# Converting streamed float64 weights: low halves moved from GpSimd to VectorE, casts as separate steps, products kept in PSUM

## The chip, the core and the metric

The kernel runs on one NeuronCore of a Trainium2 chip. The core has five instruction queues that run side by side and wait for each other through semaphores: TensorE (PE: matmuls into PSUM; PEld: its weight loads), VectorE (DVE), ScalarE (ACT), GpSimd (POOL), and SyncE (SP), which here only issues DMAs. Each queue runs its own instructions strictly in the order in which they were written. The metric is the device time of one execution in microseconds; lower is better.

## The reference, cut to what matters

A linear attention over 768 steps (a decaying 48 x 48 state per head), then two gated feed-forward layers, without any nonlinearity:

```python
# r, k, v: (4, 8, 768, 48) float32
for t in range(S):
    kt, vt, rt = (k[:, :, t], v[:, :, t], r[:, :, t])
    cur = np.einsum('bhd,bhe->bhde', u[None] * kt, vt)
    y[:, :, t] = np.einsum('bhd,bhde->bhe', rt, state + cur)
    state = w[None, :, :, None] * state + np.einsum('bhd,bhe->bhde', kt, vt)
...
x = y.transpose(0, 2, 1, 3).reshape(3072, 384)
x = ((x @ w_a) * (x @ w_b)) @ w_out          # w_a, w_b: 384 x 1536, w_out: 1536 x 384
out = ((x @ w1) * (x @ w2)) @ w3 @ w_out2    # w1, w2: 384 x 1024, w3: 1024 x 1024, w_out2: 1024 x 384
```

r, k, v, w and u arrive as float32, the seven weight matrices as float64.

## The kernel before, in words

**Precision.** A product of two float32 matrices is made of three fast matmuls: each operand is split into a high part (`hi`, the value rounded to fp32r, a cast) and a low part (`lo` = value - `hi`), and hi\*hi + lo\*hi + hi\*lo is summed in PSUM. So every weight and every intermediate needs a cast (ScalarE) and a subtraction.

**Conversion of weights (class `Stream`).** A weight arrives as float64 seen as pairs of 32-bit words, in jobs of 128 x 512 elements. The DMA (SP, L83) brings a job into a staging buffer `stg_t`; three VectorE instructions make a float32 of it in a buffer `cvt`: L98 (`shift`), L114 and L117 (`begin`). Then ScalarE casts it to `hi` (L136) and a subtraction gives `lo` (L137): on GpSimd for weights, on VectorE for the jobs that bring a float32 intermediate `m_d` back. Two more ScalarE instructions per job, Square (L121) and Sign (L139), each with an accumulator read, check the range of the values. `step()` is `finish()` of the oldest begun job (cast, low part, Sign, then the DMA of the next job), and `begin()` of the next one (L114, then L98 of the job behind it, L117, Square). `AHEAD` staging buffers are in flight. 61 jobs are float64 weights: 27 in the first stage (18 of w_a and w_b, `wab`, and 9 of w_out, `wout` and `wo`), the other 34 (`w12`, `wo2`, `w3`) from the last block of the first layer on.

**Stages.** Step 0 is the attention over the first 128 positions of the four batches (units u = 0 to 3; functions with `_0`). Then comes the first feed-forward layer in six blocks q of 512 tokens: for each of 12 feature tiles f TensorE makes a (9 matmuls, L635), b (9, L635) and, one f later, m (9 matmuls, L686 to L688, with `w_out`). Between them `merge` puts, as `side`, the attention of the next 128 positions (`unit_slots`: scores L367 and L383, `a_evac` L389, `a_diag` L395, `y_mm` L414/L419, `s_mm` L480), and as `late` the conversion steps: in block q = 0 the wab and wo jobs, in the last block the w12, wo2 and w3 jobs. The second layer runs over the same six blocks with w1/w2, and w3 @ w_out2 folded into one matrix (`fold`, L783).

**Per feature tile (`ab_slots`).** ScalarE copies a from PSUM to `g` (L654); VectorE multiplies it with b in PSUM (L660, result back into `g`, SBUF); ScalarE casts `g` to `gh` (L661); VectorE makes `gl` = `g` - `gh` (L666). TensorE's m waits for `gh` and `gl`. a and b live in three PSUM buffers `ab`. On GpSimd run the attention's elementwise products: `rk` (L321, L325), `kn` and `k` (L356), state decay `s` (L486), `pr` (L345, L347), from the third block on also `rbl` (L336) and `ktl` (L340).

**What sets the order.** The order on each queue is that of the Python code; `merge` spreads `side` and `late` evenly over the main slots. `STEPS_U`, `STEPS_K` and `TAIL` say how many conversion steps stand at each point of step 0. `st.split(n)` makes steps at once until the weights that TensorE needs next are there.

Of the kernel before, what the change touches and what calls it, by code (L numbers as in the profile page):

```python
# [23 lines left out]
DM = H * D  # L24
# [18 lines left out]
STEPS_K = (0, 2, 1, 0)  # L43
# [14 lines left out]
class Stream:  # L58
# [7 lines left out]
    AHEAD = 3  # L66

    def __init__(self, nc, stg, chk, small):
        self.nc, self.stg, self.chk, self.small = nc, stg, chk, small
        self.jobs, self.tiles = [], {}  # L70
        self.issued = self.shifted = self.begun = self.done = self.n64 = 0

    def add(self, src, dst, lo_eng=None):

        self.jobs.append((src, dst, lo_eng or self.nc.vector))
        return len(self.jobs)
# [13 lines left out]
    def shift(self):  # L90

        n = self.shifted
        if n == self.issued:
            return
        if self.jobs[n][0].dtype == I64:
            w = self.tiles[n].bitcast(I32).rearrange("p (n t) -> p n t", t=2)
            f = self.stg.tile([128, 512], I32, name="cvt", bufs=3)
            self.nc.vector.tensor_scalar(out=f, in0=w[:, :, 1], scalar1=3, scalar2=0x3FFFFFFF,  # L98
                                         op0=ALU.logical_shift_left, op1=ALU.bitwise_and)
            self.tiles[n] = (self.tiles[n], f)  # L100
        self.shifted += 1

    def begin(self):
# [7 lines left out]
        if self.jobs[n][0].dtype == I64:  # L111
# [43 lines left out]
def rwkv_moe_kernel(ctx, tc, rkT, nat, wu, wab, wout, w12, w3T, wo2, r_in, k_in, v_in, w_in, u_in, out):  # L155
# [10 lines left out]
    with tc.manual_schedule():  # L166
# [58 lines left out]
        def add_wab(i):  # L225
# [374 lines left out]
        for u in range(B):  # L600
# [10 lines left out]
            steps(STEPS_U[u])  # L611
            if u == 2:
# [25 lines left out]
        def ab_slots(x, wget, keep):  # L638
# [17 lines left out]
            def evac_b():  # L656
# [64 lines left out]
        def add_wo2(i):  # L721
# [5 lines left out]
            for j in range(3):  # L727
                s = slice(j * 512, (j + 1) * 512)
                st.add(flat(wo2)[:, i * 1536 + j * 512:][:, :512], lambda s=s: dst(s), nc.gpsimd)

        def add_w3(i):
# [5 lines left out]
            for j in range(2):  # L737
                s = slice(j * 512, (j + 1) * 512)
                w3_ready[i] = st.add(flat(w3T[i])[:, s], lambda s=s: dst(s), nc.gpsimd)

        lag, late = [], []
        for q in range(NB):
# [10 lines left out]
            if q == 0:  # L753
                late = [step] * (len(st.jobs) - st.begun + 1)
                late += [lambda: None] * (len(late) // LATE)
            if q == NB - 1:
# [7 lines left out]
                late = [step] * (len(st.jobs) - st.begun + 1)  # L764
# [65 lines left out]
        for q in range(NB):  # L830
# [29 lines left out]
            merge(main, [], late=[step] * (24 if q == 0 else 4) + [lambda: None] * (0 if q == 0 else 2))  # L860
# [254 lines left out]
```

## Time and profile before

| what | value |
|---|---|
| time, median of three runs (lowest to highest) | 942.9 us (940.86 to 945.25) |
| the profiled execution: its time / its span in the trace | 940.6 us / 938.9 us |
| TensorE busy, of the span | 898.6 us, 96% |
| VectorE / ScalarE / GpSimd busy | 478.8 / 344.0 / 306.5 us |
| chain that ended last, by engine | TensorE 80%, VectorE 11%, DMA 4%, issue 3% |
| mean granted TensorE clock | 0.979 |

The profiled execution lies 2.3 us below the median. The busy shares are means over stages that differ: in the page's 40 slices VectorE shows 7 to 9 tenths in the first six slices (up to about 140 us), mostly 4 to 5 over the next sixteen, 7 again from about 516 to 610 us, and 2 to 3 at the end. TensorE shows less than 9 in the first six slices and twice between 540 and 610 us, and the granted clock dips there too.

### The profile page before, as it was taken

How to read it: one execution, taken by the hardware profiler on the slowest of the kernel's cores; microseconds unless marked ns; L12 is line 12 of the kernel's file. 1: busy time of each engine (PE TensorE's matmuls, PEld its weight loads, DVE VectorE, ACT ScalarE, POOL GpSimd, SP SyncE). 2: the span in 40 equal slices, each digit the busy share in tenths (PEclk: the TensorE clock that was granted, in tenths of full speed). 3: DMA queues.
4: the chain of work that ended last, by engine and by line, in shares of the span. 5: the costliest groups of instructions: out<-in, count | busy, mean ns of one | idle time of the engine just before them, and what ended most of it. 6: DMA issues, size and time to landing. Idle time of an engine off the chain costs nothing.

```text
span 938.9 us, 12503 instructions
## 1 busy us (share of the span) xinstructions
PE 898.6 (96%) x4898; PEld 766.0 (82%) x4898; DVE 478.8 (51%) x684; ACT 344.0 (37%) x721; POOL 306.5 (33%) x245
## 2 busy tenths in 40 slices
PE   7778889999999999999999989899999999999997
PEld 7656678888888888888888867799988888888886
DVE  8799994545344544454442777765322222323222
ACT  4555653322322232223221775755422222222221
POOL 4566766555355626543420342322200000000000
PEclk9789889999999999999999999999999999999999
DMA  9534532212212211122102435443110010100001
GB/s 276 170 115 149 165 112 62 79 46 79 61 60 75 64 59 65 46 62 80 45 1 84 146 124 159 140 157 106 34 45 23 35 35 34 34 34 1 34 1 37
DMA packets 26065, 73.56 MB, mean 78 GB/s; under 512 B 3152, under 2 KB 7376, under 8 KB 26000
## 3 DMA queue, kind: packets, MB, share of 16 engines
q1 hardware_dynamic: 26000, 72.70, 24.6%
q8 instruction: 40, 0.66, 0.3%
q14 instruction: 25, 0.20, 0.1%
HBM read 61.28 MB, written 9.44 MB: 75 GB/s over the span
## 4 chain that ended last, share of the span: by engine, by line
PE 80%; DVE 11%; DMA 4%; issue 3%; ACT 1%; SPq 0%; DVEq 0%
PE ab L635 45%; PE m L686 4%; PE m L687 4%; PE m L688 4%; PE at L783 4%; DVE cvt L114 3%; PE o L807 3%; PE o L806 3%; PE o L808 3%; DVE cvt L117 2%; PE at L419 2%; PE at L414 2%; DVE cvt L98 1%; DMA stg_t<-in_wout_dram 1%; DVE gl L666 1%
## 5 line engine op out<-in xcount | busy, mean ns | idle before, releaser
L660 DVE TENSOR_TENSOR g<-g,ab 128x512 f32<-128x512 f32 x120 | 82.2, 685 | 269.1 <-PE ab L635 261.3
L635 PE MATMUL ab<-xt,w12h 128*128 128x512 f32 x576 | 177.5, 389 | 0.0
L661 ACT CAST gh<-g 128x512 fp32r<-128x512 f32 x120 | 74.5, 621 | 263.4 <-DVE g L660 263.4
L654 ACT COPY g<-ab 128x512 f32<-128x512 f32 x120 | 70.1, 584 | 247.4 <-PE ab L635 246.9
L666 DVE TENSOR_TENSOR gl<-g,gh 128x512 fp32r<-128x512 f32 x120 | 107.1, 893 | 65.0 <-ACT gh L661 65.0
L635 PEld LDWEIGHTS ab<-xt,w12h 128*128 128x128 f32 x576 | 107.5, 188 | 18.9
L635 PE MATMUL ab<-xt,w12l 128*128 128x512 f32 x288 | 112.0, 389 | 0.0
L687 PE MATMUL m<-gl,woh 128*128 128x512 f32 x216 | 86.4, 400 | 9.0 <-DVE gl L666 9.0
L686 PE MATMUL m<-gh,woh 128*128 128x512 f32 x216 | 87.3, 404 | 1.3 <-ACT gh L661 1.3
L336 POOL TENSOR_TENSOR rbl<-rk,rbh 48x512 fp32r<-48x512 f32 x32 | 49.3, 1542 | 120.1 <-ACT rbh L329 118.9
L688 PE MATMUL m<-gh,wol 128*128 128x512 f32 x216 | 85.2, 395 | 0.0
L635 PEld LDWEIGHTS ab<-xt,w12l 128*128 128x128 f32 x288 | 54.0, 188 | 11.2
L114 DVE SCALAR_TENSOR_TENSOR cvt<-stg_t,cvt 128x512 int32<-128x512 int32 x61 | 59.2, 970 | 0.3
L687 PEld LDWEIGHTS m<-gl,woh 128*128 128x128 f32 x216 | 41.3, 191 | 19.5 <-DVE gl L666 11.6
L117 DVE SCALAR_TENSOR_TENSOR cvt<-stg_t,cvt 128x512 int32<-128x512 int32 x61 | 54.5, 893 | 0.3
L686 PEld LDWEIGHTS m<-gh,woh 128*128 128x128 f32 x216 | 41.2, 191 | 12.4 <-ACT gh L661 3.3
L635 PE MATMUL ab<-xt,wab1h 128*128 128x512 f32 x144 | 47.0, 409 | 2.5 <-ACT wab1h L136 2.5
L688 PEld LDWEIGHTS m<-gh,wol 128*128 128x128 f32 x216 | 41.3, 191 | 8.7
L395 DVE COPY_PREDICATED a_sc<-ident,dg 128x512 f32<-128x512 int32 x40 | 46.3, 1197 | 0.0
L635 PE MATMUL ab<-xt,wab0h 128*128 128x512 f32 x144 | 45.3, 396 | 0.8 <-ACT g L654 0.8
L635 PE MATMUL ab<-xt,wab3h 128*128 128x512 f32 x144 | 45.9, 400 | 0.0
L635 PE MATMUL ab<-xt,wab2h 128*128 128x512 f32 x144 | 45.8, 400 | 0.0
(283 smaller groups left out, 1805.8 us busy)
## 6 DMA issues: line engine op xcount, KB each, us to landing
natt<-in_nat_dram SPq DMA_DIRECT2D x20, 576.0 KB, 5.0
rk<-in_rkT_dram SPq DMA_DIRECT2D x24, 448.0 KB, 4.2
stg_t<-in_wab_dram SPq DMA_DIRECT2D x18, 512.0 KB, 3.6
stg_t<-in_w3T_dram SPq DMA_DIRECT2D x16, 512.0 KB, 3.6
stg_t<-in_w_dram SPq DMA_DIRECT2D x12, 512.0 KB, 3.7
stg_t<-in_wout_dram SPq DMA_DIRECT2D x9, 512.0 KB, 3.5
m_d<-m_sb SPq DMA_DIRECT2D x18, 256.0 KB, 2.3
stg_t<-m_d SPq DMA_DIRECT2D x18, 256.0 KB, 2.6
```

Of the source, the lines that this page charges most:

```text
L114: nc.vector.scalar_tensor_tensor(out=f, in0=w[:, :, 1], scalar=-0x40000000, in1=f, op0=ALU.bitwise_and, op1=ALU.bitwise_or)
L117: nc.vector.scalar_tensor_tensor(out=f, in0=w[:, :, 0], scalar=29, in1=f, op0=ALU.logical_shift_right, op1=ALU.bitwise_or)
L336: eng.tensor_tensor(out=l, in0=rf_t[u][a:e], in1=h, op=ALU.subtract)
L395: nc.vector.copy_predicated(out=a_t[u][:, 4 * hf:4 * hf + 4, :], mask=ident.bitcast(I32).rearrange("p (o n) -> p o n", o=1).to_broadcast([ ...
L635: mm(ps, lhsT=w[i][:, k, cs], rhs=x[:, j, k, :], start=(n == 0), stop=(n == 3 * KD - 1))
L654: nc.scalar.copy(out=t["g"], in_=t["a"])
L660: nc.vector.tensor_tensor(out=g, in0=g, in1=t["b"], op=ALU.mult)
L661: nc.scalar.copy(out=gh, in_=g)
L666: nc.vector.tensor_tensor(out=gl, in0=t["g"], in1=gh, op=ALU.subtract)
L686: mm(m_ps[q][k], lhsT=wh[:, j, cs], rhs=gh, start=(f == 0), stop=False)
L687: mm(m_ps[q][k], lhsT=wh[:, j, cs], rhs=gl, start=False, stop=False)
L688: mm(m_ps[q][k], lhsT=wl[:, j, cs], rhs=gh, start=False, stop=(f == NF1 - 1))
```

## The change

Five things change.

1. In `Stream`, the low part of every job is made on VectorE (the argument that named an engine is gone). The 61 subtractions of the weights (L137) leave GpSimd.
2. Cast and Square become a step of their own, `cast()`, that stands behind each `step()` in the lists; `finish()` calls it only where it has not been made. `finish()` is now the low part and Sign.
3. `a*b` is written back into b's PSUM buffer; `gh` and `gl` are made from there.
4. Four staging buffers instead of three, and two `cvt` buffers instead of three.
5. In step 0, the loads of `k_0`, of `u_bc`, and of `rk` and `natt` for units 4 and 5 no longer stand ahead of all conversions' loads; `later_loads(u)` issues them behind units 0, 2 and 3. `STEPS_K` moves one step from unit 1 to unit 3.

```diff
-STEPS_K = (0, 2, 1, 0)
+STEPS_K = (0, 1, 1, 1)
...
-    AHEAD = 3
+    AHEAD = 4
...
-    def add(self, src, dst, lo_eng=None):
-
-        self.jobs.append((src, dst, lo_eng or self.nc.vector))
+    def add(self, src, dst):
+
+        self.jobs.append((src, dst))
...
-            f = self.stg.tile([128, 512], I32, name="cvt", bufs=3)
+            f = self.stg.tile([128, 512], I32, name="cvt", bufs=2)
...
+        self.begun += 1
+
+    def cast(self):
+
+        nc, n = self.nc, self.cast_
+        if n == self.begun:
+            return
+        hi, lo = self.jobs[n][1]()
+        if self.jobs[n][0].dtype == I64:
+            t, f = self.tiles[n]
+            f = f.bitcast(F32)
+            nc.scalar.copy(out=hi, in_=f)
             sq = self.stg.tile([128, 512], BF16, name="sq", bufs=1)
             high = t.bitcast(F32).rearrange("p (n t) -> p n t", t=2)[:, :, 1]
             nc.scalar.activation(out=sq, in_=high, func=ACTF.Square, accum_out=self.chk[:, self.n64, 0:1])
-            self.tiles[n] = (f.bitcast(F32), sq, self.n64)
+            self.tiles[n] = (f, hi, lo, sq, self.n64)
             self.n64 += 1
         else:
-            self.tiles[n] = (self.tiles[n], None, None)
-        self.begun += 1
+            f = self.tiles[n]
+            nc.scalar.copy(out=hi, in_=f)
+            self.tiles[n] = (f, hi, lo, None, None)
+        self.cast_ += 1
...
-        _, dst, eng = self.jobs[self.done]
-        t, sq, n = self.tiles.pop(self.done)
-        hi, lo = dst()
-        nc.scalar.copy(out=hi, in_=t)
-        eng.tensor_tensor(out=lo, in0=t, in1=hi, op=ALU.subtract)
+        if self.done == self.cast_:
+            self.cast()
+        f, hi, lo, sq, n = self.tiles.pop(self.done)
+        nc.vector.tensor_tensor(out=lo, in0=f, in1=hi, op=ALU.subtract)
...
-        nc.sync.dma_start(out=u_bc, in_=u_in.rearrange("(o h) d -> o (h d)", o=1).to_broadcast([128, DM]))
-        for u in range(B):
-            nc.sync.dma_start(out=k_0[:, u, :], in_=nat[u, :, 1, :])
-        for u in (B, B + 1):
-            load_rk(u)
-            load_nat(u)
+
+        def later_loads(u):
+            if u == 0:
+                for b in range(B):
+                    nc.sync.dma_start(out=k_0[:, b, :], in_=nat[b, :, 1, :])
+            elif u == 2:
+                load_rk(B)
+                nc.sync.dma_start(out=u_bc, in_=u_in.rearrange("(o h) d -> o (h d)", o=1).to_broadcast([128, DM]))
+                load_nat(B)
+            elif u == 3:
+                load_rk(B + 1)
+                load_nat(B + 1)
...
             for _ in range(n):
                 step()
+                st.cast()
...
             steps(STEPS_U[u])
+            later_loads(u)
...
-                nc.vector.tensor_tensor(out=g, in0=g, in1=t["b"], op=ALU.mult)
-                nc.scalar.copy(out=gh, in_=g)
+                nc.vector.tensor_tensor(out=t["b"], in0=g, in1=t["b"], op=ALU.mult)
+                nc.scalar.copy(out=gh, in_=t["b"])
...
-                nc.vector.tensor_tensor(out=gl, in0=t["g"], in1=gh, op=ALU.subtract)
+                nc.vector.tensor_tensor(out=gl, in0=t["b"], in1=gh, op=ALU.subtract)
...
-                late = [step] * (len(st.jobs) - st.begun + 1)
+                late = [step, st.cast] * (len(st.jobs) - st.begun + 1)
```

Three places in the instruction order follow; the second is shown on two engines. The first is SP's queue in the first microseconds, from the third staged job on (`stg_t` are staged weights, `k_96` is `k_0`). Before:

```order
L83 DMA stg_t<-in_wab_dram 128x512
L260 DMA u_bc<-in_u_dram 128x384
L262 DMA k_96<-in_nat_dram 128x384 x4
L189 DMA rk<-in_rkT_dram 112x1024
L198 DMA natt<-in_nat_dram 128x1152
L189 DMA rk<-in_rkT_dram 112x1024
L198 DMA natt<-in_nat_dram 128x1152
L83 DMA stg_t<-in_wout_dram 128x512 x3
```

After:

```order
L83 DMA stg_t<-in_wab_dram 128x512
L83 DMA stg_t<-in_wout_dram 128x512
L277 DMA k_96<-in_nat_dram 128x384 x4
L83 DMA stg_t<-in_wout_dram 128x512
L202 DMA rk<-in_rkT_dram 112x1024
L280 DMA u_bc<-in_u_dram 128x384
L211 DMA natt<-in_nat_dram 128x1152
L83 DMA stg_t<-in_wout_dram 128x512
L202 DMA rk<-in_rkT_dram 112x1024
L211 DMA natt<-in_nat_dram 128x1152
```

The fourth and fifth staged job now stand ahead of the loads of unit 4, and `u_bc` with the loads of units 4 and 5 behind them.

The second is VectorE at the first feature tile of block q = 0 (`wab1l` is the low part of a weight, `rk` an attention operand, `dg` the attention's diagonal). Before:

```order
L325 TENSOR_TENSOR rk<-rk,tk 112x512
L660 TENSOR_TENSOR g<-g,ab 128x512
L114 SCALAR_TENSOR_TENSOR cvt<-stg_t,cvt 128x512
L98 TENSOR_SCALAR cvt<-stg_t 128x512
L117 SCALAR_TENSOR_TENSOR cvt<-stg_t,cvt 128x512
L666 TENSOR_TENSOR gl<-g,gh 128x512
```

After:

```order
L117 SCALAR_TENSOR_TENSOR cvt<-stg_t,cvt 128x512
L681 TENSOR_TENSOR ab<-g,ab 128x512
L150 TENSOR_TENSOR wab1l<-cvt,wab1h 128x512
L114 SCALAR_TENSOR_TENSOR cvt<-stg_t,cvt 128x512
L98 TENSOR_SCALAR cvt<-stg_t 128x512
L117 SCALAR_TENSOR_TENSOR cvt<-stg_t,cvt 128x512
L687 TENSOR_TENSOR gl<-ab,gh 128x512
```

The low part L150 now stands on VectorE between the product and `gl`; it needs the cast of the `cvt` that L117 finished one instruction earlier.

ScalarE at the same place (`stg_t` read by Square, `sq` by Sign, `s` the state). Before:

```order
L498 COPY s_186<-s_ps 48x4x48 x2
L661 CAST gh<-g 128x512
L136 CAST wab1h<-cvt 128x512
L139 ACTIVATE sq,chk<-sq,small 128x512
L121 ACTIVATE sq,chk<-stg_t 128x512
L654 COPY g<-ab 128x512
```

After:

```order
L152 ACTIVATE sq,chk<-sq,small 128x512
L517 COPY s_173<-s_ps 48x4x48 x2
L682 CAST gh<-ab 128x512
L130 CAST wab1h<-cvt 128x512
L133 ACTIVATE sq,chk<-stg_t 128x512
L152 ACTIVATE sq,chk<-sq,small 128x512
L675 COPY g<-ab 128x512
```

The cast of a weight still stands behind `gh`, but it is now the cast that VectorE's next instruction (L150) waits for. 
The third is VectorE over one feature tile of the last block (`w12l` is the low part of a weight of the second layer). Before:

```order
L660 TENSOR_TENSOR g<-g,ab 128x512
L666 TENSOR_TENSOR gl<-g,gh 128x512
L114 SCALAR_TENSOR_TENSOR cvt<-stg_t,cvt 128x512
L98 TENSOR_SCALAR cvt<-stg_t 128x512
L117 SCALAR_TENSOR_TENSOR cvt<-stg_t,cvt 128x512
L114 SCALAR_TENSOR_TENSOR cvt<-stg_t,cvt 128x512
L98 TENSOR_SCALAR cvt<-stg_t 128x512
L117 SCALAR_TENSOR_TENSOR cvt<-stg_t,cvt 128x512
```

After (the tile numbers of `w12l` as printed):

```order
L681 TENSOR_TENSOR ab<-g,ab 128x512
L150 TENSOR_TENSOR w12l_4275<-cvt,w12h_4274 128x512
L114 SCALAR_TENSOR_TENSOR cvt<-stg_t,cvt 128x512
L98 TENSOR_SCALAR cvt<-stg_t 128x512
L117 SCALAR_TENSOR_TENSOR cvt<-stg_t,cvt 128x512
L687 TENSOR_TENSOR gl<-ab,gh 128x512
L150 TENSOR_TENSOR w12l_4275<-cvt,w12h_4274 128x512
L114 SCALAR_TENSOR_TENSOR cvt<-stg_t,cvt 128x512
L98 TENSOR_SCALAR cvt<-stg_t 128x512
L117 SCALAR_TENSOR_TENSOR cvt<-stg_t,cvt 128x512
```

One of the two conversions of the tile now stands between the product and `gl`, and each conversion is followed by a low part. TensorE's order does not change, and GpSimd's is the same without the `L137` rows.

## Rows read from the trace of the kernel before

**Rows 1.** Page: busy us (share of the span) and instructions of each engine.
```profile
PE 898.6 (96%) x4898; PEld 766.0 (82%) x4898; DVE 478.8 (51%) x684; ACT 344.0 (37%) x721; POOL 306.5 (33%) x245
```

**Rows 2.** Stretches: length, busy us (instructions) of each engine, granted clock, DMA share, GB/s.
```profile
24.00:142.00 118.00, 95.58 (x572) 76.48 (x571) 108.49 (x133) 68.38 (x166) 74.10 (x53) 0.86 0.44 140
...
142.00:518.00 376.00, 376.00 (x2175) 315.44 (x2174) 173.58 (x242) 106.60 (x196) 171.25 (x137) 1.00 0.20 60
518.00:602.00 84.00, 77.20 (x321) 60.65 (x320) 67.86 (x93) 58.25 (x134) 30.16 (x21) 0.98 0.45 144
...
602.00:939.00 337.00, 330.52 (x1630) 296.28 (x1629) 107.81 (x175) 100.54 (x200) 21.14 (x14) 1.00 0.14 46
```

**Rows 3.** Waits of PE, 24 to 142 us: line, releaser, us, times, longest.
```profile
PE at L419 <- DVE a_sc L395: 9.0, 4, 3.2
PE at L431 <- DVE a L403: 5.5, 1, 5.5
PE m L687 <- DVE gl L666: 3.6, 2, 2.2
```

**Rows 4.** DVE groups by shape, 16 to 142 us: busy us, mean ns, idle before.
```profile
L114 DVE SCALAR_TENSOR_TENSOR cvt<-stg_t,cvt 128x512 int32<-128x512 int32 x27 | 30.4, 1126 | 0.1
L117 DVE SCALAR_TENSOR_TENSOR cvt<-stg_t,cvt 128x512 int32<-128x512 int32 x27 | 24.7, 914 | 0.0
L98 DVE TENSOR_SCALAR cvt<-stg_t 128x512 int32<-128x512 int32 x27 | 22.3, 826 | 6.2 <-DMA stg_t<-in_wout_dram 5.5 <-DMA stg_t<-in_wab_dram 0.7
L666 DVE TENSOR_TENSOR gl<-g,gh 128x512 fp32r<-128x512 f32 x9 | 12.7, 1407 | 0.7 <-ACT gh L661 0.7
```

**Rows 5.** DVE L660, L666, L389, whole run: min/median/max ns; then groups, 660 to 930 us.
```profile
L660 DVE TENSOR_TENSOR g<-g,ab x120: 664/686/690, 49.4 to 928.4; 128x512 f32<-128x512 f32 x120
...
L666 DVE TENSOR_TENSOR gl<-g,gh x120: 681/691/2262, 51.8 to 929.8; 128x512 fp32r<-128x512 f32 x120
...
L389 DVE TENSOR_TENSOR a_sc<-at,mask x40: 676/688/692, 61.5 to 492.6; 128x512 f32<-128x512 f32 x40
...
L117 DVE SCALAR_TENSOR_TENSOR cvt<-stg_t,cvt 128x512 int32<-128x512 int32 x2 | 1.4, 691 | 0.0
L98 DVE TENSOR_SCALAR cvt<-stg_t 128x512 int32<-128x512 int32 x2 | 0.8, 418 | 0.0
```

**Rows 6.** Timeline of DVE and POOL at 72 us: start us, duration us, instruction.
```profile
72.69 4.04 DVE L114 SCALAR_TENSOR_TENSOR cvt<-stg_t,cvt 128x512 int32<-128x512 int32 x1
...
72.04 0.93 POOL L486 TENSOR_TENSOR s<-s,wC 112x448 f32<-112x448 f32 x1
...
73.90 1.31 POOL L137 TENSOR_TENSOR wab2l<-cvt,wab2h 128x512 fp32r<-128x512 f32 x1
75.16 1.02 POOL L347 TENSOR_TENSOR pr<-pr,natt 128x384 f32<-128x384 f32 x1
```

**Rows 7.** POOL groups by shape, 16 to 142 us (largest of seven groups of L137).
```profile
L137 POOL TENSOR_TENSOR wol<-cvt,woh 128x512 fp32r<-128x512 f32 x9 | 13.3, 1483 | 14.5 <-ACT woh L136 14.5
```

**Rows 8.** Timeline of DVE at 30 us, with the idle time before the instruction.
```profile
30.84 0.90 DVE L98 TENSOR_SCALAR cvt<-stg_t 128x512 int32<-128x512 int32 x1 [5.54 <-DMA stg_t<-in_wout_dram]
```

**Rows 9.** DVE's timeline; then stretches as in rows 2 (561: PE alone).
```profile
543.14 0.69 DVE L666 TENSOR_TENSOR gl<-g,gh 128x512 fp32r<-128x512 f32 x1 [0.69 <-ACT gh L661]
543.75 1.80 DVE L114 SCALAR_TENSOR_TENSOR cvt<-stg_t,cvt 128x512 int32<-128x512 int32 x1
...
561.07:567.23 6.16, 6.16 (x29) 1.00 0.40 107
...
543.16:550.44 7.28, 6.72 (x28) 4.99 (x28) 7.17 (x9) 5.18 (x13) 2.66 (x2) 1.00 0.46 145
```

**Rows 10.** ACT groups by shape, 518 to 602 us: busy us, mean ns.
```profile
L139 ACT ACTIVATE sq<-sq,small 128x512 bf16<-128x512 bf16 x21 | 15.1, 721 | 0.0
L121 ACT ACTIVATE sq<-stg_t 128x512 bf16<-128x512 f32 x21 | 14.0, 666 | 0.6
L136 ACT CAST w12h<-cvt 128x512 fp32r<-128x512 f32 x12 | 7.4, 620 | 3.5 <-DVE cvt L117 3.5
```

More of the change, by code (lines that the diff above doesn't have):

```diff
@@ L70, in __init__ @@
         self.jobs, self.tiles = [], {}
-        self.issued = self.shifted = self.begun = self.done = self.n64 = 0
-    def add(self, src, dst, lo_eng=None):
-        self.jobs.append((src, dst, lo_eng or self.nc.vector))
+        self.issued = self.shifted = self.begun = self.cast_ = self.done = self.n64 = 0
+    def add(self, src, dst):
+        self.jobs.append((src, dst))
         return len(self.jobs)
@@ L231, in add_wab @@
             for k in range(KD):
-                wab_ready[i] = st.add(wab[i, :, k, :], lambda k=k: dst(k), nc.gpsimd)
+                wab_ready[i] = st.add(wab[i, :, k, :], lambda k=k: dst(k))
         def add_wout(i):
@@ L241, in add_wout @@
                 s = slice(j * 512, (j + 1) * 512)
-                wo_ready[i] = st.add(flat(wout[i])[:, s], lambda s=s: dst(s), nc.gpsimd)
+                wo_ready[i] = st.add(flat(wout[i])[:, s], lambda s=s: dst(s))
         def add_w12(i):
@@ L246, in add_w12 @@
             for k in range(KD):
-                w12_ready[i] = st.add(w12[i, :, k, :], lambda k=k: [t[:, k, :] for t in w12_t[i]], nc.gpsimd)
+                w12_ready[i] = st.add(w12[i, :, k, :], lambda k=k: [t[:, k, :] for t in w12_t[i]])
         for i in range(6):
@@ L728, in add_wo2 @@
                 s = slice(j * 512, (j + 1) * 512)
-                st.add(flat(wo2)[:, i * 1536 + j * 512:][:, :512], lambda s=s: dst(s), nc.gpsimd)
+                st.add(flat(wo2)[:, i * 1536 + j * 512:][:, :512], lambda s=s: dst(s))
         def add_w3(i):
@@ L738, in add_w3 @@
                 s = slice(j * 512, (j + 1) * 512)
-                w3_ready[i] = st.add(flat(w3T[i])[:, s], lambda s=s: dst(s), nc.gpsimd)
+                w3_ready[i] = st.add(flat(w3T[i])[:, s], lambda s=s: dst(s))
         lag, late = [], []
@@ L763, in rwkv_moe_kernel @@
                     add_w3(i)
-                late = [step] * (len(st.jobs) - st.begun + 1)
+                late = [step, st.cast] * (len(st.jobs) - st.begun + 1)
             merge(main, side, len(main) - (END_0 if q == 0 else 5), late)
@@ L859, in rwkv_moe_kernel @@
             st.issue()
-            merge(main, [], late=[step] * (24 if q == 0 else 4) + [lambda: None] * (0 if q == 0 else 2))
+            merge(main, [], late=[step, st.cast] * (24 if q == 0 else 4) + [lambda: None] * (0 if q == 0 else 4))
         for q, f in lag2:
```

## The prediction

> **What bounds the kernel now.** I read the page's busy times first, then the stretches, then the waits of TensorE, and only then VectorE's groups and its timeline. TensorE is busy for 898.6 of 938.9 us [rows 1], so 40 us at most can come from filling its gaps. The stretches say where the gaps are [rows 2]: between 142 and 518 us TensorE is busy for 376.00 of 376.00 us, and between 602 and 939 us for all but 6.5 us, which lie at the end and not in the change. What is left is 118 − 95.6 = 22.4 us between 24 and 142 us (stage 1 below) and 84 − 77.2 = 6.8 us between 518 and 602 us (stage 2): the two stretches in which weights are converted. There the clock is also granted below full, 0.86 and 0.98 in the mean [rows 2]. [...]
>
> In stage 1 TensorE waits for VectorE: for the attention's matrix (9.0 and 5.5 us) and for `gl` (3.6 us) [rows 3]. VectorE is busy for 108.5 of 118 us [rows 2]. It is the bound there, and what a change is worth is the change of VectorE's own time.
>
> Much of VectorE's busy time is waiting that the profile shows as long instructions. L117 takes 691 ns and L98 418 ns where GpSimd does nothing, and `gl` 681 at its shortest [rows 5]; between 16 and 142 us they take 914, 826 and 1407, and L114 takes 1126 [rows 4]. The timeline shows why: an L114 of 4.04 us lies beside a chain of GpSimd products and ends within 0.6 us of the chain's end [rows 6]. L660 (one operand in PSUM, the other in SBUF) never takes more than 690 ns in 120, L389 (the same) never more than 692 in 40, while `gl` (both in SBUF) reaches 2262 [rows 5]. So VectorE instructions that read SBUF alone are held up by GpSimd, those with a PSUM operand are not. [...]
>
> **The change part by part.** The sum is made against the profiled execution (940.6 us; span 938.9), which lies 2.3 us below the median of 942.9.
>
> *Stage 1, VectorE's time from 16 to 142 us.* (a) The 27 low parts of wab and wout come to VectorE. Each is like an unhindered `gl`, which lets the next instruction start 0.61 us after its own start (543.14 to 543.75) [rows 9]: 27 × 0.61 = +16.5 us. (b) The hindrance: measured less unhindered, L114 30.4 − 27 × 0.69 = 11.8 (the same operation as L117), L117 24.7 − 27 × 0.69 = 6.1, L98 22.3 − 27 × 0.418 = 11.0, `gl` 12.7 − 9 × 0.69 = 6.5; 35.4 us in all [rows 4, 5]. `gl` will read PSUM and lose its 6.5 whole. Of the other 28.9, GpSimd's low parts cause about half: they are 26 instructions in seven groups, of which the largest has 1.48 us each [rows 7]: 38 us of the 74 that GpSimd is busy there [rows 2]. So −6.5 − 15 = −21.5 us. Bounds: −16, if the remaining GpSimd products run back to back and hold VectorE up as in rows 6; −27, if they fall beside PSUM instructions. (c) The DMA: L98 waits 6.2 us [rows 4], 5.54 of it once, for the fourth job [rows 8], whose load stood behind u_bc, k_0 and units 4 and 5 in SP's queue. With four buffers and the loads behind, it is issued right after the third: −6.2 us. What SP is moved past costs nothing: unit 4's operands are needed behind the conversions of step 0, over 15 us later. (d) The new wait: a low part on VectorE needs its cast on ScalarE, and all of VectorE's queue stands behind it. Of the 27, four follow their L117 at once and wait for a whole cast, 0.62 us [rows 10]; eight have one instruction between, three of them with `gh` ahead of the cast, about 1.2 us each; the rest have two or more, where now and then a y cast stands behind Square. I take 0.35 us on average, 27 × 0.35 = +9.4; bounds 3 (all but the bare ones covered) and 14 (0.52 each). The other instructions of `cast` and Sign only change places on ScalarE, which is busy for 68 of 118 us [rows 2].
>
> Sum for stage 1: 16.5 − 21.5 − 6.2 + 9.4 = **−1.8 us**. It is a small difference of large terms; TensorE's 22.4 us of waits mostly stay. Late in its place would come the same thing, VectorE's queue.
>
> *Stage 2, 518 to 602 us.* In its 30.16 us here [rows 2] GpSimd makes nothing but low parts (the attention is done), so all hindrance goes. A feature tile is 6.16 us of TensorE work at the full clock, but took 7.28 us from `m` to `m` [rows 9]. VectorE's work in one is L660 and `gl` (1.2 us) and two conversions of 0.61 + 0.34 + 0.61 = 1.56: 4.3 us, to which rows 9 add 1.1 us of hindrance twice (L114 1.80 for 0.69) and 0.69 us of waiting for `gh`. Afterwards: 4.3 + 2 × 0.61 = 5.55 us, no hindrance, and a conversion between L660 and `gl` covers the wait for `gh`. That is below 6.16, with 0.6 us to spare, and ScalarE needs 5.18 us per tile [rows 9]. So VectorE no longer falls behind, and the 6.8 us of gaps and 1.7 us of slow clock go: **−8.5 us**. If each low part waits for a whole cast, the tile is 5.55 + 1.24 = 6.8 us, between 6.16 and 7.28, and half comes back: −4.
>
> *Edits at about nothing.* Writing the product to PSUM: no row shows VectorE writing there; the nearest is reading it, 686 ns (L660) against 691 (`gl`, SBUF alone) [rows 5], so 0, with ±0.1 us on the 21 products and as many `gl` in the two stages as bounds, ±2 us. b's buffer is held until `gl`, but TensorE's next use of it stands behind the m that needs that `gl` anyway. [...] Between 142 and 518 us a faster `gl` changes nothing, since TensorE never waits [rows 2].
>
> Sum: −1.8 − 8.5 = −10.3 us: 930.3 us against the profiled 940.6, or **932.6 us** against the median.
>
> **The rivals.** *More than that.* GpSimd's remaining products slip beside PSUM instructions (−27), and the casts are covered (+3): stage 1 is 16.5 − 27 − 6.2 + 3 = −13.7, with stage 2 −22.2, **920.7 us**. For it: `gl`, L660 and L389 are all out of GpSimd's way then. Against it: rows 6, where GpSimd's chain goes first.
>
> *Given back.* The casts come later than I count (14) and the relief is small (−16): stage 1 +8.3, stage 2 −4, +4.3, **947.2 us**, or anything about the present time. For it: ScalarE's queue also holds Square and Sign, 0.67 and 0.72 us for each job [rows 10], and a cast can stand behind either.
>
> *Slower.* One mechanism: casts that stand behind `gh` or an evacuation in ScalarE's queue, which itself waits for VectorE's product or for TensorE; each low part then stalls all of VectorE, conversions, `gl` and the attention's matrix behind it, in stage 1. With a mean wait w the whole sum is 16.5 − 21.5 − 6.2 + 27w − 8.5 = −19.7 + 27w: it turns at w = 0.73 us, about one cast with its handover, and at w = 1.1 it is +10, **953 us**. Against it: 15 of 27 have two or more instructions as cover.
>
> **How the numbers follow.** Chances: the forecast 0.50 (about 924 to 938), more 0.20, given back 0.18, slower 0.12. The range 920 to 947 reaches from the first rival to the second and leaves out the slower one and the first one's far end. Half a percent, 4.7 us, is about what a measurement of this kernel can tell from no change. Faster by over that: 0.50 + 0.20 = 0.70; within: 0.18; slower: 0.12.
>
> **What the profile would show.** Right: between 518 and 602 us no wait of TensorE for `gl` and L114 at 0.69 us; no DMA wait of L98 at 30 us; `gl` never over 0.7 us; in stage 1 L114, L117 and L98 nearer to 0.69 and 0.42, new waits of L150 for ScalarE of some 9 us, and TensorE's idle time still about 20 us. Wrong: L114 in stage 1 as long as before (the hindrance is not GpSimd's low parts), TensorE gaps in stage 2, a product into PSUM well over 0.69 us, or waits of L150 above 20 us. If VectorE's idle time in stage 1 grows and TensorE's gaps vanish, VectorE was not the bound and the gain is larger than I say.

## The result, and the profile after

The changed kernel takes 930.99 us in the median of six runs (927.3 to 933.4), the kernel before 942.8 (940.86 to 945.25) on the same chip: ratio 0.9881, 95% interval 0.9861 to 0.9901. That is 11.8 us less, where 10.3 were forecast. The profiled execution took 930.97 us (span 929.3). Its page, in the columns of [rows 1]:

```profile
PE 893.2 (96%) x4898; PEld 764.2 (82%) x4898; DVE 465.8 (50%) x745; ACT 338.6 (36%) x721; POOL 212.3 (23%) x184
```

The stretches after, as in [rows 2]:

```profile
24.00:142.00 118.00, 92.26 (x551) 73.13 (x548) 106.38 (x160) 69.27 (x170) 42.46 (x30) 0.87 0.45 142
142.00:518.00 376.00, 376.00 (x2176) 315.73 (x2175) 160.47 (x247) 103.59 (x193) 161.81 (x134) 1.00 0.21 62
518.00:602.00 84.00, 84.00 (x375) 69.90 (x375) 68.01 (x117) 64.02 (x150) 0.00 (x0) 1.00 0.49 155
```

In stage 2 TensorE is busy for 84.00 of 84.00 us and the granted clock is 1.00 in the mean. In stage 1 it is idle for 25.7 us, where it was 22.4 [rows 2]: nothing was gained there.

A stretch cut at fixed times holds different work in the two kernels, so I follow the product (L660, now L681), which is there 120 times in either. The 13th starts at 161.91 us before and at 163.43 after; from it to the 59th the distance stays at 1.52 us, so this is what stage 1 came to: **+1.5 us**. From the 60th product to the 78th the stretches are, before:

```profile
512.02:655.08 143.06, 136.26 (x620) 114.61 (x619) 97.55 (x142) 89.31 (x205) 45.01 (x30) 0.99 0.42 136
```

and after:

```profile
513.54:645.45 131.91, 131.91 (x620) 113.95 (x619) 101.02 (x174) 89.17 (x208) 0.00 (x0) 1.00 0.45 146
```

The same 620 matmuls take 131.91 us in place of 143.06: **−11.15 us** in stage 2, the whole gain. From the 78th product on the distance is constant.

VectorE's groups from 16 to 142 us, as in [rows 4]:

```profile
L114 DVE SCALAR_TENSOR_TENSOR cvt<-stg_t,cvt 128x512 int32<-128x512 int32 x27 | 23.1, 854 | 0.0
L117 DVE SCALAR_TENSOR_TENSOR cvt<-stg_t,cvt 128x512 int32<-128x512 int32 x27 | 22.2, 822 | 0.0
L98 DVE TENSOR_SCALAR cvt<-stg_t 128x512 int32<-128x512 int32 x27 | 16.9, 626 | 0.0
...
L150 DVE TENSOR_TENSOR wol<-cvt,woh 128x512 fp32r<-128x512 f32 x9 | 7.9, 882 | 3.7 <-ACT woh L130 3.5
...
L687 DVE TENSOR_TENSOR gl<-ab,gh 128x512 fp32r<-128x512 f32 x9 | 6.1, 680 | 0.7 <-ACT gh L682 0.7
```

All three conversion steps are shorter than in [rows 4], but not at the 691 and 418 ns of [rows 5]; L98 waits for no DMA. Over the whole run `gl` is never held up any more, and the product into PSUM takes 10 ns longer than in [rows 5] (min/median/max ns):

```profile
L687 DVE TENSOR_TENSOR gl<-ab,gh x120: 674/691/694, 57.3 to 920.1; 128x512 fp32r<-128x512 f32 x120
```

```profile
L681 DVE TENSOR_TENSOR ab<-g,ab x120: 678/696/702, 53.0 to 918.8; 128x512 f32<-128x512 f32 x120
```

One feature tile of stage 2 on VectorE (start, duration; the counterpart of the second piece of [rows 9]):

```profile
539.80 0.69 DVE L681 TENSOR_TENSOR ab<-g,ab 128x512 f32<-128x512 f32 x1
540.57 0.69 DVE L150 TENSOR_TENSOR w12l<-cvt,w12h 128x512 fp32r<-128x512 f32 x1
541.18 0.68 DVE L114 SCALAR_TENSOR_TENSOR cvt<-stg_t,cvt 128x512 int32<-128x512 int32 x1
541.79 0.42 DVE L98 TENSOR_SCALAR cvt<-stg_t 128x512 int32<-128x512 int32 x1
542.12 0.69 DVE L117 SCALAR_TENSOR_TENSOR cvt<-stg_t,cvt 128x512 int32<-128x512 int32 x1
542.72 0.68 DVE L687 TENSOR_TENSOR gl<-ab,gh 128x512 fp32r<-128x512 f32 x1
543.50 0.69 DVE L150 TENSOR_TENSOR w12l<-cvt,w12h 128x512 fp32r<-128x512 f32 x1
...
545.65 0.68 DVE L681 TENSOR_TENSOR ab<-g,ab 128x512 f32<-128x512 f32 x1
```

5.85 us from product to product, with no waiting of note: the cast of a weight starts on ScalarE as its L117 ends and is done when the product ends. TensorE needs 6.16 [rows 9], so VectorE catches up.

TensorE's waits from 24 to 142 us, as in [rows 3]:

```profile
PE s_ps L499 <- issue: 7.0, 1, 7.0
PE at L438 <- DVE a_sc L414: 6.1, 5, 2.7
PE ab L656 <- ACT xt L462: 4.2, 1, 4.2
PE at L386 <- issue: 3.5, 1, 3.5
PE m L708 <- DVE gl L687: 3.0, 3, 1.6
```

The first, third and fourth are new; what the fourth waits for stays open. ScalarE's timeline shows what the other two stand behind:

```profile
32.97 0.62 ACT L130 CAST wab0h<-cvt 128x512 fp32r<-128x512 f32 x1 [4.90 <-DVE cvt L117]
...
34.15 0.46 ACT L462 CAST xt<-at 128x384 fp32r<-128x384 f32 x1
...
41.18 0.62 ACT L130 CAST woh<-cvt 128x512 fp32r<-128x512 f32 x1 [5.86 <-DVE cvt L117]
...
44.09 0.62 ACT L130 CAST woh<-cvt 128x512 fp32r<-128x512 f32 x1 [0.79 <-DVE cvt L117]
...
45.27 1.28 ACT L517 COPY s<-s_ps 48x192 f32<-48x192 f32 x4
```

A cast made early waits in ScalarE's queue for VectorE's newest conversion; the cast of `xt` stands behind one of them, the copies that free `s_ps` behind two. (The profile names no releaser for the first wait; that it is for these copies is read from the times, and e7 below bears it out.) VectorE is slow there because GpSimd, now free of low parts, runs its products almost without a break from 27.44 to 40.6 us, for example:

```profile
36.57 1.76 DVE L114 SCALAR_TENSOR_TENSOR cvt<-stg_t,cvt 128x512 int32<-128x512 int32 x1
...
36.06 1.73 POOL L340 TENSOR_TENSOR rk<-rk,tr 112x512 f32<-112x512 f32 x1
```

### The profile page after: what moved, and what is told of

Same layout as the page of the kernel before. It is cut to its first block, busy times and chain, and to the rows that moved or that the text cites. A ratio compares the mean times of both kernels' runs of the same rounds, so it can differ in the third digit from the quotient of the medians.

```text
span 929.3 us, 12493 instructions
## 1 busy us (share of the span) xinstructions
PE 893.2 (96%) x4898; PEld 764.2 (82%) x4898; DVE 465.8 (50%) x745; ACT 338.6 (36%) x721; POOL 212.3 (23%) x184
## 4 chain that ended last, share of the span: by engine, by line
PE 85%; DVE 9%; issue 2%; ACT 2%; DMA 1%; SPq 0%; ACTq 0%; DVEq 0%
PE ab L656 49%; PE m L707 5%; PE m L708 5%; PE m L709 5%; PE at L804 4%; PE o L828 3%; PE o L829 3%; PE o L827 3%; DVE cvt L114 2%; DVE cvt L117 2%; PE at L438 2%; PE at L433 2%; DVE cvt L98 1%; PE at L829 1%; PE at L827 1%
## 5 line engine op out<-in xcount | busy, mean ns | idle before, releaser
L681 DVE TENSOR_TENSOR ab<-g,ab 128x512 f32<-128x512 f32 x120 | 83.4, 695 | 276.2 <-PE ab L656 274.9
L682 ACT CAST gh<-ab 128x512 fp32r<-128x512 f32 x120 | 70.3, 586 | 235.7 <-DVE ab L681 235.6
L687 DVE TENSOR_TENSOR gl<-ab,gh 128x512 fp32r<-128x512 f32 x120 | 82.8, 690 | 65.7 <-ACT gh L682 65.5
L656 PE MATMUL ab<-xt,wab0h 128*128 128x512 f32 x144 | 48.1, 417 | 4.2 <-ACT xt L462 4.2
L414 DVE COPY_PREDICATED a_sc<-ident,dg 128x512 f32<-128x512 int32 x40 | 47.3, 1217 | 0.0
L114 DVE SCALAR_TENSOR_TENSOR cvt<-stg_t,cvt 128x512 int32<-128x512 int32 x61 | 46.4, 760 | 0.3
L117 DVE SCALAR_TENSOR_TENSOR cvt<-stg_t,cvt 128x512 int32<-128x512 int32 x61 | 45.5, 746 | 0.3
```

The source lines that it names most:

```text
L114: nc.vector.scalar_tensor_tensor(out=f, in0=w[:, :, 1], scalar=-0x40000000, in1=f, op0=ALU.bitwise_and, op1=ALU.bitwise_or)
L117: nc.vector.scalar_tensor_tensor(out=f, in0=w[:, :, 0], scalar=29, in1=f, op0=ALU.logical_shift_right, op1=ALU.bitwise_or)
L414: nc.vector.copy_predicated(out=a_t[u][:, 4 * hf:4 * hf + 4, :], mask=ident.bitcast(I32).rearrange("p (o n) -> p o n", o=1).to_broadcast([ ...
L656: mm(ps, lhsT=w[i][:, k, cs], rhs=x[:, j, k, :], start=(n == 0), stop=(n == 3 * KD - 1))
L681: nc.vector.tensor_tensor(out=t["b"], in0=g, in1=t["b"], op=ALU.mult)
L682: nc.scalar.copy(out=gh, in_=t["b"])
```

## The experiments

Each is compared with the kernel before on its own chip; all ratios are time over time before. "Stage 1" is the start of the 13th product against 161.91 us, "stage 2" the further change to the 78th, "tile" the mean from the 62nd product to the 73rd, all from the one profile of each kernel. Runs e1 and e2 are the same code up to 518 us and differ by 4.2 us there, so a single stage 1 figure is good to some 4 us; the stage 2 figures of kernels with the same code there lie within 0.4 us.

| kernel | median us | ratio, 95% interval | stage 1 | stage 2 | tile |
|---|---|---|---|---|---|
| before | 940.6 to 942.8 | 1 | 0 | 0 | 7.29 |
| changed | 931.0 | 0.9881 (0.9861–0.9901) | +1.5 | −11.1 | 6.18 |
| e1 lows on GpSimd | 945.2 | 1.0033 (1.0019–1.0048) | +11.7 | −6.0 | 6.63 |
| e2 lows on GpSimd, stage 1 | 939.3 | 0.9986 (0.9972–0.9999) | +7.5 | −11.0 | 6.19 |
| e3 late casts | 944.4 | 1.0041 (1.0027–1.0055) | +3.3 | +0.9 | 7.32 |
| e4 product in SBUF | 928.9 | 0.9869 (0.9847–0.9890) | +4.9 | −10.7 | 6.22 |
| e5 three `cvt`, three `stg_t` | 933.2 | 0.9918 (0.9894–0.9943) | −0.1 | −6.2 | 6.60 |
| e6 e5, lows on GpSimd | 935.5 | 0.9949 (0.9928–0.9969) | +0.3 | −5.5 | 6.67 |
| e7 copies first | 930.8 | 0.9892 (0.9848–0.9937) | −1.0 | −11.0 | 6.20 |
| e8 e5, low one job later | 933.8 | 0.9925 (0.9898–0.9952) | −4.5 | −2.9 | 6.72 |
| e9 casts alone | 943.2 | 1.0027 (1.0015–1.0039) | +6.4 | −3.6 | 6.59 |
| e10 lows alone | 945.6 | 1.0050 (1.0034–1.0066) | +4.2 | +1.1 | 7.27 |
| e11 loads first | 930.3 | 0.9882 (0.9860–0.9903) | +3.4 | −10.8 | 6.21 |
| e12 copies first, SBUF | 931.2 | 0.9900 (0.9874–0.9926) | −1.1 | −10.9 | 6.20 |

### e1 and e2: low parts back on GpSimd

```diff
-        nc.vector.tensor_tensor(out=lo, in0=f, in1=hi, op=ALU.subtract)
+        eng = nc.vector if sq is None else nc.gpsimd
+        eng.tensor_tensor(out=lo, in0=f, in1=hi, op=ALU.subtract)
```

e2 takes `nc.gpsimd` only for `n < 27`.

> The changed kernel (931.0 us) with one part undone: the 61 low parts of the weights are on GpSimd again; everything else is as changed. Theory: the whole gain is that GpSimd no longer holds VectorE up in the second conversion stage, so it is lost: products of the last block again some 7.3 us apart in place of 6.0, total 940 to 946 us. Rival: the earlier casts and the fourth staging buffer made the gain, and where the low part stands doesn't matter: 929 to 934 us, products 6.0 us apart.

> The changed kernel (931.0 us) with the 27 low parts of the first conversion stage (wab and wout) on GpSimd again and the 34 of the second stage on VectorE. Theory: in the first stage the 27 low parts on VectorE cost as much of its time as the relief from GpSimd gives back (the changed kernel stands 1.5 us behind the kernel before at 156 us), so the time stays within 3 us, 928 to 934, and the gain of the second stage, 11.1 us, stays whole. Rival: the relief in the first stage is worth several us and was only masked by the late start (first product 3.6 us later): then this is slower by over 4 us, 935 to 940.

e1 measured 945.2, in the theory's range, but not by its cause: a tile takes 6.63 us and not 7.3, so stage 2 keeps 6.0 of its 11.1 us, and the larger part of the loss is in stage 1. VectorE's timeline of e1 in stage 2:

```profile
545.18 0.69 DVE L682 TENSOR_TENSOR ab<-g,ab 128x512 f32<-128x512 f32 x1
545.78 0.68 DVE L114 SCALAR_TENSOR_TENSOR cvt<-stg_t,cvt 128x512 int32<-128x512 int32 x1
547.65 0.43 DVE L98 TENSOR_SCALAR cvt<-stg_t 128x512 int32<-128x512 int32 x1 [1.19 <-POOL w12l L151]
...
551.06 0.43 DVE L98 TENSOR_SCALAR cvt<-stg_t 128x512 int32<-128x512 int32 x1 [1.19 <-POOL w12l L151]
```

L114 (0.68 us) and L98 (0.43) take as long here as in the tile of the changed kernel above (0.68 and 0.42); L98 waits for the low part on GpSimd to free one of only two `cvt` buffers, 1.19 us twice per tile. e2 (939.3) misses the theory's range and falls into the rival's, for the same reason, which neither named: in stage 1 its L98 waits 18.6 us for low parts. Two buffers are enough only because the low part left GpSimd.

### e3 and e10: the low part on VectorE behind a late cast

e3 is the changed kernel with `st.cast()` out of `steps` and of the three `late` lists, so that `finish()` makes each cast:

```diff
                 step()
-                st.cast()
...
-                late = [step, st.cast] * (len(st.jobs) - st.begun + 1)
+                late = [step] * (len(st.jobs) - st.begun + 1)
```

e10 is the kernel before with one edit:

```diff
-        eng.tensor_tensor(out=lo, in0=t, in1=hi, op=ALU.subtract)
+        nc.vector.tensor_tensor(out=lo, in0=t, in1=hi, op=ALU.subtract)
```

> The changed kernel (931.0 us) without the casts as a step of their own: each cast is made right before its low part, as in the kernel before; low parts stay on VectorE. Theory: every low part then waits for a whole cast, 0.62 us and its handover, where 27 of them waited 6.9 us in all in the first stage: first stage 27 x 0.7 - 6.9 = +12 at most, less the 3.6 us that the start loses to casts that stand ahead of the state's copies; second stage 5.55 + 2 x 0.7 = 6.95 us per tile against 6.0, a loss of some 8 us: total 940 to 950 us. Rival: VectorE has slack enough at both places and the cast's place is worth little: 929 to 934 us.

> The kernel before (941 to 943 us) with the other part alone: the 61 low parts of the weights on VectorE, each still right behind its cast, all else as before. Theory (each low part waits for a whole cast, 0.62 us and its handover, and that takes away what the relief from GpSimd gives): 940 to 948 us, L150's waits for ScalarE at 0.6 us or more each in the second stage. Rival, the theory of the forecast (the relief is worth more than the waits): 932 to 937 us.

944.4 and 945.6: both in the theory's range, and in both the whole gain of stage 2 is gone. In e3 the late cast costs 12.0 us there, more than the some 8 expected, and only 1.8 in stage 1. VectorE in e10:

```profile
552.48 0.68 DVE L660 TENSOR_TENSOR g<-g,ab 128x512 f32<-128x512 f32 x1
554.36 0.69 DVE L137 TENSOR_TENSOR w12l<-cvt,w12h 128x512 fp32r<-128x512 f32 x1 [1.21 <-ACT w12h L136]
...
556.51 0.68 DVE L666 TENSOR_TENSOR gl<-g,gh 128x512 fp32r<-128x512 f32 x1
...
559.42 0.68 DVE L660 TENSOR_TENSOR g<-g,ab 128x512 f32<-128x512 f32 x1
```

and TensorE:

```profile
557.25 0.51 PE L687 MATMUL m<-gl,woh 128*128 128x512 f32 x1 [2.88 <-DVE gl L666]
...
558.40 0.63 PE L687 MATMUL m<-gl,woh 128*128 128x512 f32 x1
558.83 0.63 PE L688 MATMUL m<-gh,wol 128*128 128x512 f32 x1
```

No VectorE instruction is held up (GpSimd does nothing here; from 518 to 602 us L114 takes 685 ns in the mean and L98 420), but the weight's cast stands behind `gh` on ScalarE; its low part waits 1.21 us, `gl` and the next product wait with it, and a tile is 6.94 us in this place. Behind TensorE's wait of 2.88 us the matmuls start every 0.43 us, up to 560.5 us, where those in a row before it start every 0.23. The mean granted clock is 0.86 from 552 to 564 us and 0.79 from 600 to 608 us. I estimate from that some 3.4 us of work lost (0.14 × 12 + 0.21 × 8), where the kernel before lost 1.7 (0.21 × 8, at 0.79 from 552 to 560 us).

### e9: the casts alone

The changed kernel with parts 1, 3, 4 and 5 undone; what is left of the change is `cast()` as a function of its own and

```diff
                 step()
+                st.cast()
...
-                late = [step] * (len(st.jobs) - st.begun + 1)
+                late = [step, st.cast] * (len(st.jobs) - st.begun + 1)
```

> The kernel before (941 to 943 us) with one part of the change alone: cast and Square as a step of their own behind each conversion; low parts of the weights on GpSimd, three staging and three conversion buffers, the product in SBUF, the loads of step 0 early, all as before. Theory that the runs so far point to (the cast made early is the part that shortens the second stage, wherever the low part stands; the late cast cost 13 us with the low part on VectorE): second stage 5 to 9 us shorter, first stage about as before: 933 to 938 us. Rival, the theory of the forecast (GpSimd's hold on VectorE is what goes, so that the low part must leave GpSimd): no gain, 939 to 944 us.

943.2, in the rival's range; yet stage 2 is 3.6 us shorter, less than the 5 to 9 of the theory, and stage 1 longer. VectorE in stage 2:

```profile
546.00 0.68 DVE L114 SCALAR_TENSOR_TENSOR cvt<-stg_t,cvt 128x512 int32<-128x512 int32 x1
547.36 0.76 DVE L98 TENSOR_SCALAR cvt<-stg_t 128x512 int32<-128x512 int32 x1 [0.68 <-DMA stg_t<-in_w_dram]
```

GpSimd beside it:

```profile
546.21 1.62 POOL L151 TENSOR_TENSOR w12l<-cvt,w12h 128x512 fp32r<-128x512 f32 x1 [1.62 <-ACT w12h L130]
```

With three staging buffers each load now comes too late (17.8 us of such waits of L98 from 518 to 602 us), and L98 is held until GpSimd's low part is over. Why stage 1 is longer stays open. Neither of the two parts makes the kernel faster alone. The fourth staging buffer helps them but is no condition: e5 below has both parts and three staging buffers, and takes 7.4 us less than the kernel before.

### e5, e6, e8: three conversion buffers

These have three `cvt` and three `stg_t`, with the load issued behind the cast:

```diff
-    AHEAD = 4
+    AHEAD = 3
...
-            f = self.stg.tile([128, 512], I32, name="cvt", bufs=2)
+            f = self.stg.tile([128, 512], I32, name="cvt", bufs=3)
...
-        while self.issued < min(len(self.jobs), self.done + self.AHEAD):
+        while self.issued < min(len(self.jobs), self.cast_ + self.AHEAD):
...
         self.cast_ += 1
+        self.issue()
...
         self.done += 1
-        self.issue()
```

e6 adds e1's edit; e8 makes `finish()` of a job after `begin()` of the next:

```diff
-        self.finish()
-        self.begin()
+        n = self.begun
+        self.begin()
+        if self.done < n:
+            self.finish()
```

> The changed kernel (931.0 us) with three conversion buffers and three staging buffers; the next job's load is issued behind the cast and Square in place of behind the low part, so as many loads stand ahead as in the changed kernel. Low parts on VectorE. It is the base for the next run. Theory: with the low part on VectorE the second conversion buffer never waits, so the third is worth nothing: 929 to 933 us. Rival: conversion buffers do bind, 925 to 928 us; or a load comes late, 935 us and more.

> The run before with the 61 low parts of the weights on GpSimd. With two conversion buffers L98 waited some 20 us in each stage for a low part on GpSimd to free its buffer; a third takes that wait away and leaves only what GpSimd's instructions do to VectorE's. Theory (the hold-up by GpSimd is what the move takes away): L114 and L117 in the second stage back at 0.85 to 0.95 us in place of 0.69, second stage 3 to 8 us longer, first stage some 5 us longer: 938 to 945 us. Rival (it was the buffer): 929 to 934 us, as its base.

> The kernel with three conversion buffers, with each low part written one conversion later: behind L117 of the next job in place of ahead of its L114. Its cast has then had a whole conversion, 1.6 us, to be done. Theory (the waits of L150 for its cast, some 7 us in the first stage, are VectorE's own time lost there): those waits fall below 2 us, and the time is 3 to 6 us shorter, 925 to 928 us. Rival (weights come later to TensorE, which then waits for them, or the time goes into another wait of VectorE): 930 to 935 us.

e5, 933.2, lies just above its theory's range: stage 1 is as in the changed kernel, stage 2 is 5 us longer, and L98 waits 4.0 us for its loads there. e6 (935.5) falls between its cases; its interval overlaps that of e5, so with a third `cvt` the place of the low part is worth 2.3 us in the medians and not surely anything. In stage 2 of e6 L117 takes 682 ns, L114 756 and L98 687 (425 in e5): GpSimd holds up a conversion by some 0.33 us, about half of the 0.63 in the kernel before. But both e5 and e6 also wait for loads there, L98 for 4.0 and 16.9 us, so the pair doesn't show what the low part's place is worth in stage 2 where loads come in time. In stage 1 the conversions of e6 are held up by 29.3 us (28.9 in the kernel before), and those of e5 by 13.6; yet both end the stage alike (+0.3 and −0.1): what VectorE gains by the move it spends on the low parts. e8, 933.8, is the rival's number, with both mechanisms in the trace. Its VectorE groups, 16 to 142 us:

```profile
L98 DVE TENSOR_SCALAR cvt<-stg_t 128x512 int32<-128x512 int32 x27 | 16.4, 606 | 4.3 <-DMA stg_t<-in_wab_dram 4.3
...
L151 DVE TENSOR_TENSOR wol<-cvt,woh 128x512 fp32r<-128x512 f32 x9 | 7.2, 800 | 0.0
```

and 518 to 602 us:

```profile
L98 DVE TENSOR_SCALAR cvt<-stg_t 128x512 int32<-128x512 int32 x19 | 8.1, 426 | 13.3 <-DMA stg_t<-in_wo_dram 6.7 <-DMA stg_t<-in_w_dram 5.1 <-DMA stg_t<-in_w3T_dram 1.1
```

The low part's waits are gone and stage 1 stands 4.4 us ahead of its base, as the theory said (about the scatter of one profile); stage 2 gives 3.3 us of that back to loads that come late.

### e4, e7, e11, e12: single parts

e4 keeps the product in `g`:

```diff
-                nc.vector.tensor_tensor(out=t["b"], in0=g, in1=t["b"], op=ALU.mult)
-                nc.scalar.copy(out=gh, in_=t["b"])
+                nc.vector.tensor_tensor(out=g, in0=g, in1=t["b"], op=ALU.mult)
+                nc.scalar.copy(out=gh, in_=g)
...
-                nc.vector.tensor_tensor(out=gl, in0=t["b"], in1=gh, op=ALU.subtract)
+                nc.vector.tensor_tensor(out=gl, in0=t["g"], in1=gh, op=ALU.subtract)
```

e11 undoes part 5 (the diff of the change, its loads and `STEPS_K`, read backwards):

```diff
-STEPS_K = (0, 1, 1, 1)
+STEPS_K = (0, 2, 1, 0)
...
-            later_loads(u)
```

e7 moves the state's copies of units 0 and 1 ahead of four conversion steps; e12 is e4 and e7:

```diff
-STEPS_K = (0, 1, 1, 1)
-TAIL = (1, 2)
+STEPS_K = (0, 1, 1, 0)
+TAIL = (0, 4)
```

> The changed kernel (931.0 us) with the product a*b kept in SBUF, as in the kernel before. Theory: gl (both operands in SBUF) is held up by GpSimd again, but only where GpSimd works: in the first stage 9 of them at some 0.3 us, between 142 and 518 us without any wait of TensorE, and not at all from 518 us on: 0 to +3 us, 931 to 934; product back at 686 ns from 695. Rival: the product into PSUM costs more than it brings (it holds b's bank longer): 927 to 930 us.

> The changed kernel (931.0 us) with the two state copies of units 0 and 1 (and the matmuls that they read) ahead of the last four conversion steps of step 0, where they stood behind two of them: on ScalarE they no longer stand behind casts that wait for VectorE. TensorE's wait of 7.0 us at 39 to 46 us for the copies' buffer then goes. Theory (VectorE's queue is the bound of the first stage, the first product stands at its place in it): 930 to 932 us, the time as before. Rival (the late start of 3.6 us is this wait): 926 to 928 us.

> The changed kernel (931.0 us) with the loads of step 0 in their old order (u_bc, k_0 and units 4 and 5 ahead of the conversions' loads but the first three) and the old places of the four conversion steps. Theory: L98 waits again some 5 us for the fourth job's load, at a time when VectorE's queue is the bound: 933 to 938 us. Rival (the wait is covered, since the first product waits for other things): 929 to 932 us.

> The changed kernel (931.0 us) with the state's copies ahead of the last four conversion steps of step 0, and with the product kept in SBUF: the two single edits that came out at or a little below the changed kernel (930.8 and 928.9 us). Theory (both are worth nothing that can be told from the scatter of 927 to 933 us): 928 to 932 us. Rival (they are worth 1 to 3 us, together more): 925 to 928 us.

All four agree with the changed kernel within the intervals; e11's theory (933 to 938) missed, and its 930.3 is the rival's number. e4's 928.9 lies in the rival's range, but also among the changed kernel's own runs (927.3 to 933.4), and e12 doesn't bear it out. e7 took the wait for `s_ps` away, and TensorE waits one step later instead:

```profile
53.28 1.22 PE L656 MATMUL ab<-xt,wab0h 128*128 128x512 f32 x2 [10.22 <-ACT g L675]
```

Its first product starts at 53.47 us (53.01 in the changed kernel): at its place in VectorE's queue, whatever TensorE does. In e11 the load's wait is back (16 to 142 us):

```profile
L98 DVE TENSOR_SCALAR cvt<-stg_t 128x512 int32<-128x512 int32 x27 | 13.1, 487 | 4.6 <-DMA stg_t<-in_wout_dram 4.6
```

but L98 itself takes 3.8 us less than the 16.9 above, about as much as it waits. Not at once: up to the first product it takes 5.6 us in either kernel (nine times), and that product starts at 58.41 us, 5.4 later than in the changed kernel. Of the eighteen after it, four take 1.2 to 1.5 us in the changed kernel and none here, and the 13th product is only 1.9 us later. Why GpSimd is less in L98's way there I can't say. No version here is surely faster than the changed kernel.

## Why the prediction was right, and where its steps were not

**The bound** was read rightly: stage 2's gaps could go whole, and in stage 1 VectorE's queue sets the pace (e7 shows that directly for the first product).

**The total** owes something to chance: in the profiled executions (−9.6 us for −10.3) stage 2 gave 2.7 us more than the forecast and stage 1 3.3 us less.

**Stage 2** came to −11.1, not −8.5. The term was mis-sized: I added idle time (6.8) and slow clock (1.7), but TensorE's busy time for the same 620 matmuls fell by 136.26 − 131.91 = 4.35 us. No run shows the 1.7 us as a loss of its own; what the trace before shows in its place is a granted clock of 0.79 from 552 to 560 us, with matmuls 0.43 us apart where it is 0.50, and 0.21 × 8 = 1.7 us is an estimate from that. TensorE waits nine times in this stretch before, never after:

```profile
PE m L687 <- DVE gl L666: 5.5, 5, 2.5
PE m L686 <- ACT gh L661: 1.3, 4, 0.4
```

Behind a wait at 580 us the matmul shows 0.50 us of busy time, and the next one starts 0.33 us after it, where those in a row start every 0.23 us:

```profile
580.29 0.50 PE L687 MATMUL m<-gl,woh 128*128 128x512 f32 x1 [0.23 <-DVE gl L666]
580.62 0.39 PE L688 MATMUL m<-gh,wol 128*128 128x512 f32 x1
580.85 0.39 PE L686 MATMUL m<-gh,woh 128*128 128x512 f32 x1
```

The tile of [rows 9], with two waits, is busy for 6.72 us where 6.16 are enough: 0.28 us for each wait that is no work. By this one tile nine waits make some 2.5 us, and with the 1.7 estimated for the clock that is 4.2 of the 4.35. VectorE's tile was put at 5.55 and took 5.85.

The reason given was half of it. "All hindrance goes" is true, but e10 has no hindrance in stage 2 either and gains nothing, and e1, with the low parts on GpSimd and early casts, keeps 6.0 us: the early cast decides with it. What the low part's place is worth by itself, with early casts, is not shown: in e1 the two `cvt` buffers bind, in e5 and e6 the loads. For the case that every low part waits for its cast I had a tile of 6.8 us, of which half would come back; e10 shows 6.94 in one place, 7.27 in the mean, and nothing came back, part of it by the clock. This is the mechanism of the rival "Slower", which put it in stage 1; e3 shows it in stage 2, and the cast as a step of its own is what keeps it off. And I gave the fourth staging buffer only the wait at 30 us, where L98 waits for loads in stage 2 without it (4.0 us in e5, 13.3 in e8, 17.8 in e9, 0.2 in the changed kernel).

**Stage 1**, VectorE's time from 16 to 142 us, term by term:

| term | forecast | measured |
|---|---|---|
| (a) 27 low parts | +16.5 | +16.5, and 2.8 in which they are held up themselves (seven groups, 21.4 us busy, less 27 × 0.69) |
| (b) hindrance | −21.5 | 4.5 (L114) + 3.6 (L117) + 5.6 (L98) + 0 (`gl`) = 13.7 left of 35.4: −21.7 |
| (c) DMA | −6.2 | −6.2 in the trace; worth nothing by e11 |
| (d) cast waits | +9.4 | 3.5 + 1.5 + 1.2 + 0.7 = +6.9 |

The sum is −1.7 against −1.8, but TensorE ended the stage 1.5 us later, not 1.8 earlier. Some 2 us were not in the sum at all: VectorE's waits for ScalarE's casts of `xt` (L463 1.7 for 0.6 us, L476 1.9 for 1.2), and eight L414 of 8.1 us in place of 6.9, less 0.8 that `rk` (L344) gained. The rest is within the scatter of single profiles, and against the medians (−11.8 in all) stage 1 is −0.7; which it is stays open. e5 and e6, which differ in the place of the low part alone, bear (b) out: 29.3 − 13.6 = 15.7 us for the 15 that I took. But the 6.5 us of `gl` were not PSUM's doing alone: in e4, which reads it from SBUF, nine `gl` take 7.0 us where they took 12.7, so 5.7 of them went with the low parts.

What failed is (c) as a gain: I counted that wait in full, and with it back (e11) the time is the same, with L98 held up less later on. What I didn't see is the start: the early casts put ScalarE behind VectorE, and GpSimd's products close up, and the first product starts 3.6 us later than before (53.01 for 49.44; 50.85 with late casts, e3). How much of it each of the two makes is not shown. The fourth product is already 1.3 us ahead (80.21 for 81.55).

**PSUM.** The product's +10 ns is a tenth of the bound that I gave (0.1 us); `gl` with one operand in PSUM takes 691 ns, as from SBUF in [rows 5]. ScalarE's cast gains: `gh` takes 587 ns from PSUM (621 from SBUF). With the low parts on VectorE this part of the change is worth nothing that can be told (e4).

**The signs in the profile** came as listed but for one: no wait for `gl` and L114 at 684 ns in stage 2, no DMA wait at 30 us, `gl` at most 694 ns, waits of L150 at 6.9 us for some 9. TensorE's idle time in stage 1 grew to 25.7 us, where about 20 were expected.

## What to carry to other kernels

Moving an instruction onto the engine that bounds a stage pays only if its operand is ready (in e10 the low part waited 1.21 us for its cast): move the producer first, and test the parts singly, because here two parts that each lost 2 to 5 us alone took 11 us off stage 2 together, in a kernel with one staging buffer more. Price a stalled loop by its time per round against the round without stalls, not by idle time, since busy time next to a wait is not all work (6.72 us busy in a tile of 6.16). A wait taken away ahead of a full queue only moves down the queue (e7: without the wait for `s_ps`, TensorE waits 10.22 us one step later).

## What the runs showed of the hardware that was not expected

In e9's rows VectorE and GpSimd hold each other up in both directions: GpSimd's low part, begun 0.21 us after L114, takes 1.62 us, where the shortest of its group takes 1.29, and the L98 that begins beside it takes 0.76 for 0.42 and ends 0.3 us after it. The 128x512 product takes VectorE 696 ns in the median where it is written to PSUM and 686 where it is written to SBUF; its cast takes ScalarE 587 ns from PSUM and 621 from SBUF.
